# The first stage of an attention and gated-MLP kernel on one core, its order of work changed

## The chip, the cores and the metric

The kernel runs on one core of a Trainium2 chip. The core has a matrix engine (TensorE, PE in the profile), a vector engine (VectorE, DVE), an activation engine (ScalarE, ACT), a general engine (GpSimd, POOL) and a synchronising engine (SyncE, SP) that here only issues transfers. Each engine takes its instructions in the order in which they were written; semaphores hold an instruction back until what it needs is there. The metric is the device time of one execution in microseconds, lower is better.

## The reference

For 8 batches, 8 heads, 576 positions and 64 numbers per head: attention in which a position sees its neighbours up to 32 away, 8 global positions see everything, and everything sees them; then a gated feed-forward block over all 4608 tokens.

```python
scores = scale * np.matmul(q, k.transpose(0, 1, 3, 2))
mask = np.abs(pos[:, None] - pos[None, :]) <= 32
mask = mask | is_global[:, None] | is_global[None, :]
attn = softmax(np.where(mask, scores, -1e9))
x = (attn @ v).transpose(0, 2, 1, 3).reshape(4608, 512)
ffn = gelu(x @ w_gate) * (x @ w_val) @ w_out          # 512 -> 1536 -> 512
out = x + sigmoid(x @ w_res) * ffn
```

## The kernel before

The 4608 tokens are cut into 9 chunks of 512, and each batch into 9 windows of 64 positions, so a chunk has 8 windows. From chunk to chunk the feed-forward matmuls of one chunk run on TensorE while the attention of the next is made beside them. Only the first chunk has nothing to run beside: the first 28 us or so of the kernel are its attention, and the change is there. The schedule is written out by hand; the order of the calls in the source is the order on each engine.

What happens in this first stage, with the names used in the code:

- SyncE's queue (and two transfers on ScalarE's) loads q and k of batch 0 in five parts (head pairs 0 to 3 and a tail called -1), then V in five parts, then the weights as pieces of 512 KB (`load_piece`), each into a free staging place. SyncE issues in order and waits for earlier transfers as it goes.
- `cast_raw` turns a part of q or k into bfloat16: parts 0 and 1 on VectorE (k) and ScalarE (q), the rest on GpSimd. `turn_pair` transposes it on TensorE (`tk`, `tq` in PSUM) and copies it out (`kt` on VectorE, `qt` on ScalarE).
- `first_masks` makes `isg` in PSUM, and from it `hide`, which a matmul adds to the scores; `other_masks` makes `nong`, `row_masks` makes `maskr` (two instructions) from `far`, `nong` and `hot`. `one_hot` tiles (`picked`, `held_end`, `picked_end`) pick the global rows out of k and q by matmuls (`pick`); `own`, `vgb` and `gt` are constants and padding for the global rows.
- `first_scores(quad, pp)` makes two banks of local scores (four windows, two head pairs) and takes their exponential into `pt` (`weigh`, ScalarE).
- `global_scores`, `global_exp` and `global_rows` make the scores of the 8 global rows, their exponential (`ptg`, `gt`), multiply `gt` by `maskr` (VectorE), sum over all keys into `sn`, and spread the sum by head into `vgs` (VectorE, two instructions for batch 0).
- V is cast by GpSimd into `ve` (five parts); `vo` is the same shifted by 64 rows, made by copies between partition halves.
- `local_values(0, t)` multiplies `pt` with V for two windows; `global_values` adds the global part from `gt` and `vgs`; `norm` divides (VectorE) into `xtok`; `turn_x` transposes (`tx`) and copies to `xt` (ScalarE for t = 0, 1, 2, VectorE for t = 3).
- `begin(t, js)` multiplies the 128 columns of token block t with the first two column blocks of the gate and value weights; after it the feed-forward loop runs with 512 columns at a time.
- GpSimd casts the weight pieces 0, 1, 2 ... (`cast_piece`) as they land; piece 0 is for gate, piece 1 for value.

Of the kernel before, what the change touches and what calls it, by code (L numbers as in the profile page):

```python
# [13 lines left out]
ALU = mybir.AluOpType  # L14


def view(t, p0, pn, off, dims):

    step = t.ap[0][0]
    return bass.AP(tensor=t.tensor, offset=t.offset + p0 * step + off, ap=[[step, pn]] + dims)  # L20
# [3 lines left out]
def kernel(  # L24
# [12 lines left out]
    nc = tc.nc  # L37
    B, H, S, D = q.shape
# [99 lines left out]
    def staged(n):  # L138
        return slots[turn_of[n]].rearrange("p (a b) -> p a b", b=pieces[n][1].shape[2])
# [1 line left out]
    def load_piece(n):  # L141
        nc.sync.dma_start(staged(n), pieces[n][0])

    def cast_piece(n, copy):
        copy(pieces[n][1], staged(n))  # L145

# [102 lines left out]
    def zero_v(i, eng):  # L251
        eng.memset(ve[i][:, :, :, D:VG], 1.0)
        eng.memset(ve[i][0:32, 0, :, :], 0.0)
        eng.memset(ve[i][96:128, 4, :, :], 0.0)

    def zero_gt(i, eng):
        eng.memset(gt[i][:, 0:64], 0.0)
        eng.memset(gt[i][:, 64 + S:128 + S], 0.0)
# [87 lines left out]
    picked = const.tile([128, RPP, NG], BF16, name="picked", tag="picked")  # L346
    picked_end = const.tile([128, RPP, H, NG], BF16, name="picked_end", tag="picked_end")
    held_end = const.tile([128, RPP, NG], BF16, name="held_end", tag="held_end")
    for n, t in enumerate((picked, held_end)):
        nc.vector.tensor_tensor(t, view(gall, 0, 128, 0, [[0, RPP], [1, NG]]),  # L350
                                view(place, 0, 128, RPP * n, [[1, RPP], [0, NG]]), ALU.is_equal)
    nc.vector.tensor_tensor(picked_end, view(held_end, 0, 128, 0, [[NG, RPP], [0, H], [1, NG]]),
                            view(low8, 0, 128, 0, [[0, RPP], [1, H], [0, NG]]), ALU.mult)
    nc.vector.memset(own[0][:, 0:16], 0.0)
    nc.vector.tensor_scalar(own[0][:, 16:128], ident[:, 0:112], ask_row, None, ALU.mult)
    nc.vector.tensor_scalar(own[1], ident, keys_row, None, ALU.mult)
    zero_gt(0, nc.vector)
    NWM = NW + 3
    maskw = const.tile([128, NWM, 64], BF16, name="maskw", tag="maskw")

# [19 lines left out]
    def other_masks():  # L380
        for hf, n in enumerate((256, 320)):
            nc.vector.tensor_single_scalar(nong[:, 256 * hf:256 * hf + n], isg[:, hf, 0:n], 0.5, ALU.is_lt)

    def row_masks():

        nc.vector.scalar_tensor_tensor(maskr, far, 1024.5, nong, ALU.is_gt, ALU.mult)
        nc.vector.tensor_tensor(maskr, maskr, hot, ALU.add)
# [1 line left out]

    twice = {what: const.tile([128, B // 2, 2, D], BF16, name=f"{what}gd", tag=f"{what}gd") for what in "kq"}  # L390
    vgb = const.tile([128, B // 2, VG], BF16, name="vgb", tag="vgb")
    nc.vector.memset(vgb[:, :, D:VG], 1.0)

    def double_qk(n0, n1):
        for what in "kq":
# [35 lines left out]
                             view(src[what], 64 * u, 64, off + 16 * e + 8 * u, [[32, NP], [1, NG]]))  # L431

    def spread_v(n0, n1):
        nc.vector.tensor_copy(vgb[:, n0:n1, 0:D], gath["v"][:, n0:n1, :])

    ring = {"n": 0}
# [54 lines left out]
    def global_exp(b, sg, ss):  # L491
        e = b % 2
        to = ptg[e].rearrange("k c r -> k (c r)")
        done = 0
        for part in ss:
            n = part.shape[1]
            nc.scalar.activation(to[:, done:done + n], part, ACTF.Exp, bias=0.0, scale=SCALE)
            done += n
        g = gt[e][:, 64:64 + S]
        nc.scalar.activation(g.rearrange("p (a c) -> p a c", a=2), sg[:, :, 0:288], ACTF.Exp, bias=0.0, scale=SCALE)  # L500
        nc.vector.tensor_tensor(g, g, maskr, ALU.mult)
# [20 lines left out]
                                    view(head8, 0, 128, 2 * p, [[2, n], [1, 2], [0, VG]]), ALU.mult)  # L522


    def first_scores(quad, pp):

        sc = [bank([128, 2, 4, 64], "sc") for _ in range(2)]
        for u in range(2):
            nc.tensor.matmul(sc[u], ident_big, view(hide, 0, 128, 256 * quad, [[0, 2], [1, 256]]), start=True, stop=False)
        heads(0, quad, pp, sc, False)  # L530
        for u in range(2):
            weigh(quad, pp, u, sc[u])

    def heads(c, quad, pp, sc, first):

# [9 lines left out]
    def weigh(quad, pp, u, sc, stay=False):  # L545
        mine = view(pt, 0, 128, ((4 * pp + u) * CH + 4 * quad) * 64, [[2 * CH * 64, 2], [64, 4], [1, 64]])
        nc.scalar.activation(sc if stay else mine, sc, ACTF.Exp, bias=0.0, scale=SCALE)  # L547
        return mine, sc if stay else mine
# [22 lines left out]
    def local_values(c, t):  # L571
        if split(c, t):
            pool, tag = (pss, "sc") if c else (psm, "mm")
            nds = [pool.tile([128, 512], F32, name=f"nd{hf}", tag=tag) for hf in range(2)]
            nd = None
        else:
            nd = psn.tile([128, 2, 512], F32, name="nd", tag="nd")
            nds = [nd[:, 0, :], nd[:, 1, :]]
        wins = [divmod(CH * c + 2 * t + e, NW) for e in range(2)]
        for h in range(H):  # L580
            for e, (b, i) in enumerate(wins):
                vw = ve[b % 2][:, i // 2, h, :] if i % 2 == 0 else vo[b % 2][:, i // 2, h, :]
                nc.tensor.matmul(nds[h // 4][64 * e:64 * e + 64, VG * (h % 4):VG * (h % 4) + VG],  # L583
                                 pt[:, h, 2 * t + e, :], vw, start=(h % 4 == 0), stop=False)
        return nd, nds, wins
# [149 lines left out]
            cast_raw(p, what, POOL)  # L735
    for p in (0, 1):
        if p:
            for what in "kq":
                turn_pair(0, p, what)
        for what in "kq":  # L740
            pick(p, what)
    other_masks()
    zero_v(0, nc.vector)
    first_scores(0, 0)
    for p in (-1, 2, 3):
        for what in "kq":
            if p == 3:
                pick(p, what)
            else:
                turn_pair(0, p, what)  # L750
        if p == 3:
            spread_picked()
        for what in "kq":
            if p == 3:
                turn_pair(0, p, what)
            else:
                pick(p, what)
        if p < 0:
            ACT(found_end, isg[:, 0, 320:448])
            first_scores(1, 0)  # L760
    sg, ss = global_scores(0)
    for c in range(2):
        cast_v(0, c, POOL)
    POOL(vo[0][64:128, 0:1, :, :], ve[0][0:64, 1:2, :, :])
    DVE(vo[0][0:64, 0:2, :, :], ve[0][64:128, 0:2, :, :])
    spread_v(0, 1)
    row_masks()
    global_exp(0, sg, ss)
    first_scores(0, 1)
    cast_v(0, 2, POOL)  # L770
    POOL(vo[0][64:128, 1:2, :, :], ve[0][0:64, 2:3, :, :])
    for c in (3, 4):
        cast_v(0, c, POOL)
    POOL(vo[0][64:128, 2:4, :, :], ve[0][0:64, 3:5, :, :])
    first_scores(1, 1)
    begun_v = [local_values(0, t) for t in range(2)]
    global_rows(0)
    ACT(vo[0][0:64, 2:4, :, :], ve[0][64:128, 2:4, :, :])

    nc.scalar.activation(none, none, ACTF.Gelu, bias=0.0, scale=1.0)  # L780
    for n in range(4):
        cast_piece(n, POOL)
        if n < 2:
            load_piece(10 + n)
        else:
            load_raw(1, "kq"[n - 2], 0, nc.sync)
        if n == 1:
            fill(band, 1.0, [([[-1, 64]], 1, 0, ALU.is_ge, 0.0), ([[1, 64]], -1, 64, ALU.is_ge, 0.0)])
# [15 lines left out]

    values(0, 2)
    turn_x(0, 0)
    values(0, 3)
    turn_x(0, 1)
    begin(0, (0,))
    turn_x(0, 2)  # L810
    begin(0, (1,))
    begin(1)
# [201 lines left out]
```

## Time and profile before

| what | value |
|---|---|
| median of 3 runs | 385.8 us (385.33 to 386.08) |
| the profiled execution | 385.43 us, of which the span of the core is 383.7 us |
| TensorE busy | 370.2 us, 96% of the span |
| VectorE, ScalarE, GpSimd busy | 200.7, 169.6 and 168.9 us |
| slices of TensorE's busy share (40 of 9.6 us) | the first is 3 tenths, the last 6, nearly all others 9 or more |

The profile is one execution. Times in it count from the start of the span. In the timeline a row has the start, the length, the engine, the line of the source, the operation, the tiles written and read, the shape and how many instructions were merged; a bracket at its end is the time that the engine stood idle before it and what ended that idleness. In the table by stretches each engine has its busy time in that stretch.

### The profile page before, as it was taken

How to read it: one execution, taken by the hardware profiler on the slowest of the kernel's cores; microseconds unless marked ns; L12 is line 12 of the kernel's file. 1: busy time of each engine (PE TensorE's matmuls, PEld its weight loads, DVE VectorE, ACT ScalarE, POOL GpSimd, SP SyncE). 2: the span in 40 equal slices, each digit the busy share in tenths (PEclk: the TensorE clock that was granted, in tenths of full speed). 3: DMA queues.
4: the chain of work that ended last, by engine and by line, in shares of the span. 5: the costliest groups of instructions: out<-in, count | busy, mean ns of one | idle time of the engine just before them, and what ended most of it. 6: DMA issues, size and time to landing. Idle time of an engine off the chain costs nothing.

```text
span 383.7 us, 8470 instructions
## 1 busy us (share of the span) xinstructions
PE 370.2 (96%) x3332; PEld 185.1 (48%) x3332; DVE 200.7 (52%) x467; ACT 169.6 (44%) x291; POOL 168.9 (44%) x203
## 2 busy tenths in 40 slices
PE   3989989999999999999999999999999999999996
PEld 2574555445544554455444544454445444444444
DVE  7767674536723573447434744564446534553322
ACT  4763685336333543355334633372338233723311
POOL 7877683868255624661366128712501210121012
PEclk9999999999999999999999999999999999999999
DMA  8999999799949943999399939994990410041002
GB/s 242 251 375 365 246 334 219 165 179 162 106 112 148 202 72 104 129 193 106 92 141 172 125 98 127 188 97 126 105 165 4 109 57 0 3 113 53 0 29 83
DMA packets 156810, 53.70 MB, mean 140 GB/s; under 512 B 140194, under 2 KB 147234, under 8 KB 156770
## 3 DMA queue, kind: packets, MB, share of 16 engines
q1 hardware_dynamic: 80832, 42.80, 46.8%
q0 software_dynamic: 75392, 9.84, 43.9%
q8 instruction: 26, 0.43, 0.5%
q10 hardware_dynamic: 546, 0.52, 0.4%
q14 instruction: 14, 0.11, 0.1%
HBM read 39.19 MB, written 9.44 MB: 127 GB/s over the span
## 4 chain that ended last, share of the span: by engine, by line
PE 84%; DMA 9%; SPq 3%; POOL 2%; issue 1%; DVE 0%; ACTq 0%; DVEq 0%; POOLq 0%
PE f_ps L703 24%; PE v_ps L647 22%; PE g_ps L647 22%; PE r_ps L673 8%; DMA extra<-in_moe_w_val_dram 5%; PE nd L583 3%; SPq L185 3%; PE sc L540 2%; DMA wo_t<-in_k_dram 2%; PE nd L596 2%; DMA xtok<-in_v_dram 2%; DMA ht<-in_q_dram 1%; POOL wo_t L145 1%; PE sg L478 1%; PE sg L485 1%
## 5 line engine op out<-in xcount | busy, mean ns | idle before, releaser
L656 DVE SCALAR_TENSOR_TENSOR ht<-gsb,v_ps 128x512 bf16<-128x512 bf16 x108 | 74.2, 688 | 97.5 <-PE v_ps L647 90.2
L653 ACT ACTIVATE gsb<-g_ps 128x512 bf16<-128x512 f32 x108 | 64.4, 597 | 121.9 <-PE g_ps L647 120.7
L709 POOL TENSOR_TENSOR ob<-prb,xtok 128x512 f32<-128x512 f32 x35 | 40.3, 1155 | 167.0 <-DVE prb L707 167.0
L647 PE MATMUL g_ps<-xt,wg_t 128*128 128x512 bf16 (+1 forms) x456 | 111.9, 368 | 0.0
L647 PE MATMUL v_ps<-xt,wv_t 128*128 128x512 bf16 (+1 forms) x456 | 111.9, 368 | 0.0
L703 PE MATMUL f_ps<-wo_t,ht 128*128 128x512 bf16 x420 | 97.9, 379 | 0.0
L647 PEld LDWEIGHTS <-wv_t 128*128 128x128 bf16 x456 | 43.5, 98 | 49.1
L647 PEld LDWEIGHTS <-wg_t 128*128 128x128 bf16 x456 | 43.4, 98 | 48.7
L703 PEld LDWEIGHTS <-ht 128*128 128x128 bf16 x420 | 40.4, 98 | 46.9
L681 ACT ACTIVATE rsb<-r_ps 128x512 bf16<-128x512 f32 x36 | 21.9, 611 | 66.5 <-PE r_ps L673 66.5
L707 DVE SCALAR_TENSOR_TENSOR prb<-rsb,f_ps 128x512 f32<-128x512 bf16 x35 | 24.1, 688 | 51.2 <-PE f_ps L703 50.4
L673 PE MATMUL r_ps<-wr_t,xt 128*128 128x512 bf16 x144 | 37.0, 381 | 1.0 <-ACT rsb L681 1.0
L547 ACT ACTIVATE pt<-sc 128x512 bf16<-128x512 f32 x64 | 33.3, 615 | 3.8 <-PE sc L540 3.8
L91 POOL DMA_DIRECT2D q_st<-in_q_dram x25 | 21.5, 866 | 18.2 <-DMA qt<-q_st 18.1
L99 POOL DMA_DIRECT2D ve<-in_v_dram x30 | 25.5, 866 | 0.0
L565 DVE TENSOR_TENSOR pt<-pt,maskw 128x512 bf16<-128x512 bf16 x56 | 21.9, 422 | 2.5 <-ACT pt L547 0.9
L91 POOL DMA_DIRECT2D k_st<-in_k_dram x25 | 21.2, 867 | 3.6 <-DMA kt<-k_st 2.9
L673 PEld LDWEIGHTS <-xt 128*128 128x128 bf16 x144 | 12.3, 98 | 15.8 <-issue 3.9
L583 PEld LDWEIGHTS <-pt 128*64 128x64 bf16 x576 | 11.2, 110 | 9.7 <-issue 5.0
L583 PE MATMUL nd<-ve,pt 128*64 128x65 bf16 x320 | 13.6, 196 | 0.7 <-DVE xtok L617 0.6
L617 DVE TENSOR_TENSOR xtok<-nd,rden 128x512 bf16<-128x512 f32 x20 | 13.8, 691 | 0.8
L611 DVE TENSOR_TENSOR xtok<-nd,rden 128x256 bf16<-128x256 f32 x32 | 13.6, 425 | 1.1
(174 smaller groups left out, 289.4 us busy)
## 6 DMA issues: line engine op xcount, KB each, us to landing
out_dram<-ob SPq DMA_DIRECT2D x35, 256.0 KB
vo<-ve SPq DMA_DIRECT2D x12, 260.0 KB
q_st<-in_q_dram POOLq DMA_DIRECT2D x20, 128.0 KB, 6.3
k_st<-in_k_dram POOLq DMA_DIRECT2D x20, 128.0 KB, 6.7
ve<-in_v_dram POOLq DMA_DIRECT2D x18, 128.0 KB, 7.6
wo_t<-in_k_dram SPq DMA_DIRECT2D x8, 256.0 KB
vraw<-in_q_dram SPq DMA_DIRECT2D x8, 256.0 KB
extra<-in_moe_w_out_dram SPq DMA_DIRECT2D x4, 512.0 KB
```

The lines of the kernel that those rows point to most:

```text
L91: nc.gpsimd.dma_start(dst[0:n, r, :].rearrange("p (h d) -> p h d", d=D), src[b].rearrange("h s d -> s h d")[128 * r:128 * r + n])
L99: nc.gpsimd.dma_start(t[p0:p1, c, :, 0:D], v[b].rearrange("h s d -> s h d")[s0 + p0:s0 + p1])
L547: nc.scalar.activation(sc if stay else mine, sc, ACTF.Exp, bias=0.0, scale=SCALE)
L565: nc.vector.tensor_tensor(m, x, view(maskw, 0, 128, 64 * i0, [[0, 2], [64, 4], [1, 64]]), ALU.mult)
L583: nc.tensor.matmul(nds[h // 4][64 * e:64 * e + 64, VG * (h % 4):VG * (h % 4) + VG], pt[:, h, 2 * t + e, :], vw, start=(h % 4 == 0), stop=F ...
L647: nc.tensor.matmul(held[what][:, c0:c1], w[:, kk, 128 * j:128 * j + 128], x[:, kk, c0:c1], start=(kk == 0), stop=(kk == NKT - 1))
L653: nc.scalar.activation(held["s"], held["g"], ACTF.Gelu, bias=0.0, scale=1.0)
L656: nc.vector.scalar_tensor_tensor(ht[:, j, :], held["s"], 0.5, held["v"], ALU.mult, ALU.mult)
L673: nc.tensor.matmul(r_ps, xt[c % 2][:, kk, 128 * t:128 * t + 128], wr_t[:, kk, :], start=(kk == 0), stop=(kk == NKT - 1))
L703: nc.tensor.matmul(held["f"], ht[:, j, 128 * t:128 * t + 128], wo_t[:, j, :], start=(j == 0), stop=(j == NFF - 1))
L707: nc.vector.scalar_tensor_tensor(prb, held["r"], 1.0, held["f"], ALU.add, ALU.mult)
L709: nc.gpsimd.tensor_tensor(ob, prb, xtok[c % 2][:, t, :], ALU.add)
```

## The change

In the helper `cast_piece` a range of columns can be given. The one-hot tiles for the tail, the `own` constants and the padding of `gt` become functions that are called later: after the picks of the pairs 0 and 1 and (for `own`) after `zero_v`. `other_masks` is called between the turns of pair 0 and pair 1, `row_masks` after the tail's pick, before the scores of quad 1. The exponential of `first_scores(0, 1)` is called after `global_exp`, which itself comes after the V casts and copies; the last V copy goes from ScalarE to VectorE and up ahead of `global_exp`; `global_rows(0)` comes ahead of the two `local_values`. The casts of the weight pieces 0 and 1 are cut into two halves of 128 columns. `begin(0, (0,))` moves ahead of `values(0, 3)` and `turn_x(0, 1)`.

```diff
+    def cast_piece(n, copy, n0=0, n1=None):
+        copy(pieces[n][1][:, :, n0:n1], staged(n)[:, :, n0:n1])
...
-    for n, t in enumerate((picked, held_end)):
-        nc.vector.tensor_tensor(t, view(gall, ...), view(place, ...), ALU.is_equal)
-    nc.vector.tensor_tensor(picked_end, view(held_end, ...), view(low8, ...), ALU.mult)
-    nc.vector.memset(own[0][:, 0:16], 0.0)
-    nc.vector.tensor_scalar(own[0][:, 16:128], ident[:, 0:112], ask_row, None, ALU.mult)
-    nc.vector.tensor_scalar(own[1], ident, keys_row, None, ALU.mult)
-    zero_gt(0, nc.vector)
+    def one_hot(t, n): ...            # the same is_equal
+    def one_hot_end(): ...            # held_end, then picked_end
+    def own_rows(): ...               # own[0], own[1], zero_gt(0)
+    one_hot(picked, 0)
...
-    nc.vector.memset(vgb[:, :, D:VG], 1.0)
...
     def spread_v(n0, n1):
+        if n0 == 0:
+            nc.vector.memset(vgb[:, :, D:VG], 1.0)
...
     for p in (0, 1):
         if p:
+            other_masks()
             for what in "kq":
                 turn_pair(0, p, what)
         for what in "kq":
             pick(p, what)
-    other_masks()
+    one_hot_end()
     zero_v(0, nc.vector)
+    own_rows()
     first_scores(0, 0)
...
             ACT(found_end, isg[:, 0, 320:448])
+            row_masks()
             first_scores(1, 0)
     sg, ss = global_scores(0)
...
+    spread_v(0, 1)
     DVE(vo[0][0:64, 0:2, :, :], ve[0][64:128, 0:2, :, :])
-    spread_v(0, 1)
-    row_masks()
-    global_exp(0, sg, ss)
-    first_scores(0, 1)
+    late = first_scores(0, 1, False)
...
     POOL(vo[0][64:128, 2:4, :, :], ve[0][0:64, 3:5, :, :])
+    DVE(vo[0][0:64, 2:4, :, :], ve[0][64:128, 2:4, :, :])
+    global_exp(0, sg, ss)
+    for u in range(2):
+        weigh(0, 1, u, late[u])
     first_scores(1, 1)
+    global_rows(0)
     begun_v = [local_values(0, t) for t in range(2)]
-    global_rows(0)
-    ACT(vo[0][0:64, 2:4, :, :], ve[0][64:128, 2:4, :, :])
...
     for n in range(4):
-        cast_piece(n, POOL)
+        if n < 2:
+            for j in range(2):
+                cast_piece(n, POOL, 128 * j, 128 * j + 128)
+        else:
+            cast_piece(n, POOL)
...
     values(0, 2)
     turn_x(0, 0)
+    begin(0, (0,))
     values(0, 3)
     turn_x(0, 1)
-    begin(0, (0,))
     turn_x(0, 2)
```

## Rows read from the trace of the kernel before

**Rows 1.** Busy time by stretch: length, then each engine's busy time, clock, DMA
```profile
0.00:23.70 23.70, 15.62 (x288) 10.56 (x289) 18.46 (x76) 14.54 (x26) 18.87 (x37) 1.00 1.03 269
23.70:46.90 23.20, 23.18 (x195) 13.98 (x193) 14.86 (x39) 11.31 (x21) 17.07 (x22) 1.00 1.09 330
```
**Rows 2.** Timeline of TensorE in the first stage: start, length, instruction, idle before
```profile
6.64 0.61 PE L450 MATMUL tk<-ident,k_st 128*128 128x128 bf16 x4 [0.86 <-DVE k_st L270]
...
13.60 0.40 PE L450 MATMUL tk<-ident,k_st 128*128 128x128 bf16 x4
...
15.58 0.64 PE L485 MATMUL sg<-qt,kgz 128*32 128x288 bf16 x8 [0.51 <-DVE qgz L422]
...
20.47 0.83 PE L596 MATMUL nd<-vgs,gt 128*128 128x260 bf16 x4 [0.53 <-DVE vgs L520]
...
22.86 0.22 PE L583 MATMUL nd<-ve,pt 128*64 128x65 bf16 x1 [0.55 <-DVE xtok L617]
...
24.82 0.39 PE L647 MATMUL g_ps<-xt,wg_t 128*128 128x128 bf16 x4
...
27.90 1.02 PE L647 MATMUL g_ps<-xt,wg_t 128*128 128x512 bf16 x4
```
**Rows 3.** Timeline of VectorE, the first masks and k casts
```profile
5.40 0.42 DVE L352 TENSOR_TENSOR picked_end<-held_end,low 128x256 bf16<-128x256 bf16 x1
5.75 0.40 DVE L355 TENSOR_SCALAR own<-ident,nums 128x112 bf16<-128x112 bf16 x1
...
6.17 0.42 DVE L270 CAST k_st<-wo_t 128x512 bf16<-128x512 f32 x1
...
7.16 0.53 DVE L270 CAST k_st<-wo_t 128x512 bf16<-128x512 f32 x1
```
**Rows 4.** Timeline of VectorE, from the tail's copy to the global sums
```profile
11.66 0.87 DVE L455 COPY kt<-tk 64x256 bf16<-64x256 bf16 x2
14.04 0.69 DVE L457 COPY kt<-tk 128x512 bf16<-128x512 bf16 x1 [1.50 <-PE tk L450]
...
17.02 0.75 DVE L386 SCALAR_TENSOR_TENSOR maskr<-xtok,nong 128x576 bf16<-128x576 f32 x1
17.80 0.75 DVE L387 TENSOR_TENSOR maskr<-maskr,hot 128x576 bf16<-128x576 bf16 x1
18.65 1.12 DVE L501 TENSOR_TENSOR gt<-gt,maskr 128x576 bf16<-128x576 bf16 x1
19.99 0.76 DVE L520 TENSOR_TENSOR vgs<-sn,head 128x260 bf16<-128x260 f32 x2 [0.22 <-PE sn L516]
```
**Rows 5.** Timeline of VectorE, later, beside GpSimd's weight casts and V copies
```profile
33.94 0.90 DVE L396 CAST kgd<-kgf 128x128 bf16<-128x128 f32 x1
...
52.25 0.46 DVE L501 TENSOR_TENSOR gt<-gt,maskr 128x576 bf16<-128x576 bf16 x1 [0.27 <-ACT gt L500]
```
**Rows 6.** Timeline of GpSimd: gathers, casts of q and k, V copy, weight casts, V of batch 1
```profile
4.76 1.39 POOL L327 DMA_INDIRECT vgf<-in_v_dram,idx  x1 [0.87 <-DVE ghot L337]
6.45 0.99 POOL L327 DMA_INDIRECT kgf<-in_k_dram,idx  x1 [0.30 <-issue]
...
8.70 0.62 POOL L267 CAST k_st<-wo_t 128x512 bf16<-128x512 f32 x1
...
11.49 0.61 POOL L270 CAST q_st<-ht 128x512 bf16<-128x512 f32 x1
...
18.30 1.16 POOL L774 COPY vo<-ve 64x1040 bf16<-64x1040 bf16 x1
...
21.17 1.04 POOL L145 CAST wv_t<-extra 128x1024 bf16<-128x1024 f32 x1 [0.37 <-DMA extra<-in_moe_w_val_dram]
...
33.72 1.04 POOL L145 CAST wv_t<-extra 128x1024 bf16<-128x1024 f32 x1 [0.32 <-DMA extra<-in_moe_w_val_dram]
```
**Rows 7.** Timeline of ScalarE: exponential of the global rows, copy of the first token block
```profile
17.26 0.65 ACT L500 ACTIVATE gt<-sg 128x576 bf16<-128x576 f32 x1
...
22.36 0.57 ACT L628 COPY xt<-tx 128x512 bf16<-128x512 bf16 x1
```

More of the change, by code (lines that the diff above doesn't have):

```diff
@@ L142, in load_piece @@
         nc.sync.dma_start(staged(n), pieces[n][0])
-    def cast_piece(n, copy):
-        copy(pieces[n][1], staged(n))
+    def cast_piece(n, copy, n0=0, n1=None):
+        copy(pieces[n][1][:, :, n0:n1], staged(n)[:, :, n0:n1])
     RPP = 4
@@ L348, with one_hot, one_hot_end, own_rows @@
     held_end = const.tile([128, RPP, NG], BF16, name="held_end", tag="held_end")
-    for n, t in enumerate((picked, held_end)):
+    def one_hot(t, n):
         nc.vector.tensor_tensor(t, view(gall, 0, 128, 0, [[0, RPP], [1, NG]]),
                                 view(place, 0, 128, RPP * n, [[1, RPP], [0, NG]]), ALU.is_equal)
-    nc.vector.tensor_tensor(picked_end, view(held_end, 0, 128, 0, [[NG, RPP], [0, H], [1, NG]]),
-                            view(low8, 0, 128, 0, [[0, RPP], [1, H], [0, NG]]), ALU.mult)
-    nc.vector.memset(own[0][:, 0:16], 0.0)
-    nc.vector.tensor_scalar(own[0][:, 16:128], ident[:, 0:112], ask_row, None, ALU.mult)
-    nc.vector.tensor_scalar(own[1], ident, keys_row, None, ALU.mult)
-    zero_gt(0, nc.vector)
+    def one_hot_end():
+        one_hot(held_end, 1)
+        nc.vector.tensor_tensor(picked_end, view(held_end, 0, 128, 0, [[NG, RPP], [0, H], [1, NG]]),
+                                view(low8, 0, 128, 0, [[0, RPP], [1, H], [0, NG]]), ALU.mult)
+    def own_rows():
+        nc.vector.memset(own[0][:, 0:16], 0.0)
+        nc.vector.tensor_scalar(own[0][:, 16:128], ident[:, 0:112], ask_row, None, ALU.mult)
+        nc.vector.tensor_scalar(own[1], ident, keys_row, None, ALU.mult)
+        zero_gt(0, nc.vector)
+    one_hot(picked, 0)
     NWM = NW + 3
@@ L522, in global_rows, with first_scores @@
                                     view(head8, 0, 128, 2 * p, [[2, n], [1, 2], [0, VG]]), ALU.mult)
-    def first_scores(quad, pp):
+    def first_scores(quad, pp, now=True):
         sc = [bank([128, 2, 4, 64], "sc") for _ in range(2)]
@@ L530, in first_scores @@
         heads(0, quad, pp, sc, False)
-        for u in range(2):
+        for u in range(2 if now else 0):
             weigh(quad, pp, u, sc[u])
+        return sc
     def heads(c, quad, pp, sc, first):
```

## The prediction

> **What bounds the kernel now.** I read the engine table first: TensorE is busy for 370.2 of 383.7 us, and the slices say that only the first of 9.6 us is far from full. So the whole kernel ends earlier or later by what the first stage moves TensorE's start into its unbroken work. The table by stretches says where that is: 15.62 us busy in the first 23.7 us, then 23.18 of 23.20 [rows 1]. TensorE's timeline then gives the holes of the first stage and who ended them: the first k cast (until 6.64), the spread of the global rows (until 15.58), the global sums `vgs` (until 20.47) and the division of token block 1 (until 22.86); the first 512-column matmul, at 27.90, is the mark by which I count [rows 2]. Every one of these holes ends on VectorE, which is busy 18.46 of 23.7 us [rows 1]; so I read VectorE's queue row by row, and beside it GpSimd's, because some VectorE rows are longer than their work.
>
> **A wait between VectorE and GpSimd that the change walks into.** The product of `gt` with its mask takes 0.46 us in batch 1 and 1.12 us in batch 0 [rows 4, 5]. In batch 0 it starts at 18.65 inside GpSimd's copy of V (18.30 to 19.46) and ends 0.31 us behind that copy [rows 4, 6]. The cast of `kgd`, 128 numbers a row, takes 0.90 us and ends at 34.84, 0.08 us behind GpSimd's weight cast (33.72 to 34.76) [rows 5, 6]. So a VectorE instruction that reads two tiles in SBUF, or casts from SBUF to SBUF, waits for the GpSimd instruction that runs, and does its work then. [...]
>
> **The change part by part.**
>
> *Start.* `held_end`, `picked_end`, `own` and padding leave the queue ahead of the first k cast, which now starts at 6.17 [rows 3] and could start about 5.2. That would be 0.9 us. But GpSimd's first gather runs from 4.76 to 6.15, and the `own` product inside it took 0.40 us for 112 numbers and ended with it; the second k cast (0.53 against 0.42 us) ends 0.25 us behind the second gather's end at 7.44 [rows 3, 6]. So I let the first k cast wait too and end 0.25 us behind 6.15, at 6.40 instead of 6.59: a gain of 0.2 us. Bounds: 0.2 and 0.95. [...]
>
> *The moved constants.* They now stand behind the copy of pair 1, which I place at 9.0 to 9.8, `nong` (0.8 us, moved into the hole before it) costing nothing. From 8.70 to 12.10 GpSimd casts six parts without a break, the first and the last of them in [rows 6], about 0.56 us apart. `held_end` waits for the cast that ends near 9.85 and ends at 9.9; `picked_end` waits for the next and ends at 10.7; `zero_v` runs to 11.6; `own[0]` waits to 11.8; `own[1]` for the last cast, to 12.3. So the tail's copy, at 11.66 before [rows 4], starts at 12.3: 0.6 us late. Without any wait it would be at 11.05, which is the other bound.
>
> *Row masks.* Two instructions of 0.75 us [rows 4]; the second held a wait, as its shape took 0.46 us for `gt`. Behind the tail's copy they run from 13.2 to 13.9 and, behind the V cast that the first held up, from 14.4 to 14.7. The hole that they aim at, 1.50 us before the copy at 14.04 [rows 4], starts 0.6 us later and is too short: the copy of pair 2 starts at 14.65, 0.6 us late, and with it the spread, the copy of pair 3 and the global scores, at 16.2 for 15.58 [rows 2], and the exponential of `gt`, which ends at 18.5 for 17.91 [rows 7].
>
> *What the move gives back.* VectorE has 1.5 us less in front of the `gt` product. `vgb` and the two V copies (about 1.3 us with one wait) fit before 18.5. The product starts at 18.55, again inside the GpSimd copy of V (now about 18.3 to 19.3), and ends at 19.6 for 19.77. `global_rows` ahead of `local_values`: its matmuls need the last V cast (18.0), `ptg` and a bank that the first late exponential frees (19.0); they end by 19.55, hidden under the product. So `vgs` starts at 19.64 instead of 19.99 [rows 4]: 0.35 us gained. Local values fill the time to 20.1; they need the second late exponential, 19.5, and are not late. The V copy on VectorE takes 1.06 us off ScalarE, where the load of the Gelu table hides it anyway: the copy of block 0 waits for its transposes.
>
> *`begin` ahead of `values(0, 3)`.* It is meant for the hole of 0.55 us before 22.86 [rows 2]. But it needs `xt` of block 0, which ScalarE copies from 22.36 to 22.93 [rows 7], later than the hole's end. So TensorE waits for ScalarE and then runs 0.45 us of `begin` (8 matmuls of 128 columns at 0.056), and `values(0, 3)` comes at 22.93 + 0.05 + 0.45 - 0.35 = 23.08 for 22.86. Behind it 0.45 us are saved, but the next block's copy (another 0.57 us) is then what `begin(1)` waits for: 24.75 for 24.82 [rows 2]. The move by itself costs 0.28 us; bounds: a gain of 0.45 if the copy were early, a loss of 0.45.
>
> *Weights in halves.* Four casts of 0.61 for two of 1.04 us: 0.4 us more GpSimd time at the most. The value piece lands at about 21.1 (its cast waits for it until 21.17 [rows 6]), so the halves of piece 0 hide before it, and its second half ends at 22.35, two microseconds before it is used. Nothing; if uncovered, 0.3 us. The loads of pieces 10 and 11 wait for these casts, but SyncE reaches them later, held by earlier transfers.
>
> **Sum.** -0.35 + 0.28 is -0.07; I take -0.1 us at the mark 27.90. TensorE is unbroken behind it, so it goes through. The profiled execution of 385.43 becomes 385.3; that is 0.37 below the median of 385.8, so the median becomes **385.7 us**.
>
> The clock is a bound of its own. [...] TensorE had been working since 6.64 with breaks below a microsecond when it rose, near 13.2. [...] I put 0.4 us either way.
>
> **Rivals.**
>
> *A, faster: the holes are as empty as they look.* No wait for GpSimd. Then the first k cast ends at 5.6, scores and turns come 0.9 us earlier, the masks fit before the copy of pair 2 (13.4), the `gt` product starts at 17.5, before GpSimd's copy, and `vgs` is bound by the sums at 18.4. The local values then bound (to 19.4), -1.15 us at block 0's division, +0.28 for `begin`: **384.9 us** (-0.87). For it: the bracket of 1.50 us in [rows 4], `picked_end` unstretched [rows 3]. Against it: the 1.12 and 0.90 us. A middle case belongs here, in which only the `gt` product slips in front of GpSimd's copy.
>
> *B, slower: VectorE's queue around the masks.* Same mechanism, worse order: six instructions each wait a whole GpSimd cast (0.56 us), where I let four wait, and some of them partly. Then the copy of pair 2 comes 1.6 to 1.8 us late instead of 0.6, and the chain of exponentials behind it (0.5 us each) ends at 20.6; the local values of the second half wait for it and pass `vgs`. It decides from 1.2 us late on. At 1.8 late local values end at 20.9 for 20.1, which with `begin` gives +0.9: **386.7 us**.
>
> *C: gain swallowed later.* With 0.9 us gained, the weight casts (one per 1.36 us, bound by transfers) and batch 1's V could be late. Stretch two has no break [rows 1], and its casts are ahead by more than that as I read them; if it holds, A turns into -0.4, 385.4 us, within my likeliest case's range.
>
> **How the numbers follow.** The likeliest case (with C) has 0.43 and its own range is 385.1 to 386.4. A has 0.36, B 0.21. What this kernel's measurement can tell from no change is 0.2%, 0.77 us: faster is below 385.03, slower above 386.57. The range for 8 in 10 reaches to A's 384.9 with 0.3 for the clock, and past B's 386.7 with half as much: 384.6 to 386.9, a tenth left out on either side. Chances: faster 0.36, same 0.43, slower 0.21.
>
> **What would show it.** In the changed profile: the first k cast ends near 6.4 (A: 5.6); `own[1]` and `picked_end` longer than alone; the copy of pair 2 at 14.65 (A: 13.4, B: 15.8); the `gt` product over 0.9 us and ending near GpSimd's copy's end; a wait of TensorE for ScalarE before the first `begin`; the first 512-column matmul at 27.8 (A: 27.0, B: 28.8). The prediction is wrong if that matmul moves by more than 0.8 us, or if it doesn't and the end does.

## The result and the profile after

The changed kernel takes 389.2 us (median of 6, 388.3 to 389.8) where the kernel before takes 385.9 beside it: ratio 1.0076, 95% interval 1.0052 to 1.010. That is 3.3 us slower by the medians (2.9 by the ratio, which goes by the means); the forecast was 385.7 (384.6 to 386.9), so the result lies 2.3 us outside its range. The profiled execution took 389.23 us with a span of 387.5 (385.43 and 383.7 before).

The same two stretches of the table by windows, after (columns as in [rows 1]):

```profile
0.00:23.70 23.70, 15.73 (x222) 9.75 (x224) 19.64 (x66) 11.65 (x22) 19.59 (x39) 1.00 1.03 274
23.70:46.90 23.20, 22.49 (x233) 13.66 (x226) 16.77 (x46) 10.33 (x20) 17.29 (x21) 1.00 1.08 326
```

TensorE is busy for as long in the first stretch as before (15.7 us), but gets through 222 instructions in place of 288: its work there is slower and later. TensorE's timeline, after, at the lines that answer to [rows 2]:

```profile
5.65 0.61 PE L459 MATMUL tk<-ident,k_st 128*128 128x128 bf16 x4
...
12.42 0.37 PE L423 MATMUL isg<-picked_end,k_st 128*128 128x64 bf16 x4 [1.32 <-DVE picked_end L356]
...
15.55 0.61 PE L459 MATMUL tk<-ident,k_st 128*128 128x128 bf16 x4
...
18.49 0.69 PE L494 MATMUL sg<-qt,kgz 128*32 128x288 bf16 x8 [0.63 <-DVE qgz L429]
...
24.10 0.80 PE L606 MATMUL nd<-vgs,gt 128*128 128x260 bf16 x4
...
26.62 0.38 PE L657 MATMUL g_ps<-xt,wg_t 128*128 128x128 bf16 x4 [0.67 <-ACT xt L638]
...
31.91 1.02 PE L657 MATMUL g_ps<-xt,wg_t 128*128 128x512 bf16 x4
```

Read the starts against [rows 2] as a ladder: the first transposes are 0.99 us early (5.65 for 6.64); the transposes of pair 2 are 1.95 us late (15.55 for 13.60), the global scores 2.91 (18.49), the global rows' values 3.63 (24.10), the first 512-column matmul 4.01 (31.91 for 27.90). The span ends 3.8 us late, so nothing is added behind that mark. So the early gain and 2.9 us beside it are lost between 5.7 and 18.5, and 1.1 us more from there to the mark. VectorE's timeline after, against [rows 3] and [rows 4]:

```profile
5.17 0.42 DVE L270 CAST k_st<-wo_t 128x512 bf16<-128x512 f32 x1
...
8.23 0.68 DVE L466 COPY kt<-tk 128x512 bf16<-128x512 bf16 x1
8.83 2.75 DVE L351 TENSOR_TENSOR held_end<-gall,place 128x32 bf16<-128x32 f32 x1
11.61 0.76 DVE L356 TENSOR_TENSOR picked_end<-held_end,low 128x256 bf16<-128x256 bf16 x1
...
13.35 0.38 DVE L361 TENSOR_SCALAR own<-ident,nums 128x112 bf16<-128x112 bf16 x1
...
13.64 0.65 DVE L362 TENSOR_SCALAR own<-ident,nums 128x128 bf16<-128x128 bf16 x1
...
14.28 0.83 DVE L464 COPY kt<-tk 64x256 bf16<-64x256 bf16 x2
15.15 1.06 DVE L394 SCALAR_TENSOR_TENSOR maskr<-xtok,nong 128x576 bf16<-128x576 f32 x1
16.24 0.75 DVE L395 TENSOR_TENSOR maskr<-maskr,hot 128x576 bf16<-128x576 bf16 x1
17.03 0.69 DVE L466 COPY kt<-tk 128x512 bf16<-128x512 bf16 x1
...
18.47 0.69 DVE L466 COPY kt<-tk 128x512 bf16<-128x512 bf16 x1
...
21.45 0.75 DVE L510 TENSOR_TENSOR gt<-gt,maskr 128x576 bf16<-128x576 bf16 x1
23.58 0.43 DVE L529 TENSOR_TENSOR vgs<-sn,head 128x260 bf16<-128x260 f32 x1 [1.38 <-PE sn L525]
```

`held_end`, 32 numbers a row, takes 2.75 us; it is also the first long piece in the chain of work that ended last. GpSimd's timeline after, over the same time, the first, the fifth and the last of six casts that follow each other without a break:

```profile
8.70 0.62 POOL L267 CAST k_st<-wo_t 128x512 bf16<-128x512 f32 x1
...
10.92 0.60 POOL L270 CAST k_st<-wo_t 128x512 bf16<-128x512 f32 x1
11.48 0.60 POOL L270 CAST q_st<-ht 128x512 bf16<-128x512 f32 x1
```

`held_end` starts behind the first cast's start and is done at 11.57, just past the end of the fifth cast (10.92 + 0.60); `picked_end` is done at 12.36, past the end of the sixth (12.08). So it missed four boundaries between casts. The two take 3.5 us in place of 0.6, and VectorE has hardly any free time from there to the copy of pair 2: 17.03 less the 2.9 lost is 14.1, its old 14.04. Without the wait that copy would not be late. With it, the row masks also find no hole any more (1.50 us before 14.04 in [rows 4]) and stand in the way. The copy of pair 3 comes next; in the kernel before it is

```profile
15.55 0.69 DVE L457 COPY kt<-tk 128x512 bf16<-128x512 bf16 x1
```

and after it comes at 18.47: of the 4.01 us at the mark, 2.92 are lost by this copy and 1.09 behind it.

The second part is TensorE's clock. In the trace's clock records the level 1.00 begins at 13.21 before and at 23.43 after; that is its rise. (Ahead of the first such record the clock column of the table shows 1.00 too, so there the level is read from the rows.) In rows: the four transposes at 15.55 still take 0.61 us, with starts 0.107 us apart, as at 6.64 in [rows 2], where before they took 0.40, with starts 0.056 apart, from 13.60 on. One more pair of rows, the last score work ahead of the global sums, before:

```profile
17.60 0.60 PE L529 MATMUL sc<-xt,ident_big 128*128 128x512 bf16 x2
18.14 0.41 PE L540 MATMUL sc<-qt,kt 64*128 64x64 bf16 x16
```

and after:

```profile
21.18 1.03 PE L538 MATMUL sc<-xt,ident_big 128*128 128x512 bf16 x2
22.15 0.61 PE L550 MATMUL sc<-qt,kt 64*128 64x64 bf16 x16
```

The two rows span 0.95 us before and 1.58 after. There are two such groups ahead of the sums, so 1.3 us more, and TensorE is what `vgs` waits for there (1.38 us in the row at 23.58).

### The profile page after: what moved, and what is told of

Read it like the earlier page. It is cut to its first block, busy times and chain, and to the rows that moved or that the text cites. A ratio compares the mean times of both kernels' runs of the same rounds, so it can differ in the third digit from the quotient of the medians.

```text
span 387.5 us, 8471 instructions
## 1 busy us (share of the span) xinstructions
PE 373.6 (96%) x3332; PEld 186.4 (48%) x3332; DVE 207.0 (53%) x468; ACT 168.5 (43%) x290; POOL 169.2 (44%) x205
## 4 chain that ended last, share of the span: by engine, by line
PE 86%; DVE 4%; DMA 3%; issue 2%; POOL 2%; ACT 2%; DVEq 0%; POOLq 0%
PE f_ps L713 23%; PE g_ps L657 22%; PE v_ps L657 21%; PE r_ps L683 8%; PE nd L593 3%; PE sc L550 3%; PE nd L606 2%; DMA q_st<-in_q_dram 2%; DMA kt<-k_st 1%; POOL ve L99 1%; PE sg L487 1%; PE sg L494 1%; DVE held_end L351 1%; PE sn L525 1%; PE tx L637 0%
## 5 line engine op out<-in xcount | busy, mean ns | idle before, releaser
L91 POOL DMA_DIRECT2D k_st<-in_k_dram x25 | 21.1, 865 | 4.1 <-DMA kt<-k_st 2.5
L550 PEld LDWEIGHTS <-kt 64*128 64x128 bf16 x576 | 10.4, 98 | 8.9 <-issue 6.0
L550 PE MATMUL sc<-qt,kt 64*128 64x64 bf16 x576 | 13.4, 196 | 1.3 <-DVE kt L464 1.1
```

Source lines behind the costliest of these rows:

```text
L91: nc.gpsimd.dma_start(dst[0:n, r, :].rearrange("p (h d) -> p h d", d=D), src[b].rearrange("h s d -> s h d")[128 * r:128 * r + n])
L550: nc.tensor.matmul(sc[u][:, m, n, :], kt[b % 2][64 * u:64 * u + 64, 2 * pp + m, 64 * i:64 * i + 128], qt[b % 2][64 * u:64 * u + 64, 2 * pp ...
```

## Experiments

Times are medians; each ratio is to runs of the kernel before on the same chip (385.3 to 385.6).

**The two one-hots alone.** The kernel before, `held_end` and `picked_end` moved and nothing else:

```
     other_masks()
+    one_hot_end()
     zero_v(0, nc.vector)
```

> The kernel before with one edit alone: held_end and picked_end move behind the picks of pairs 0 and 1. Theory T (GpSimd's unbroken run of casts, 8.70 to 12.1, keeps VectorE out until it ends; the late tail then breaks TensorE's work and its clock rises later): held_end lasts over 1.5 us, TensorE waits about 0.5 us for picked_end, the end is 0.5 to 3 us later than before (386.4 to 389). Rival R (each instruction waits for one cast at most; the loss is made by the row masks and by begin): held_end under 0.6 us, the end within 0.5 us of before.

Measured: 387.51, ratio 1.0047 (1.0016 to 1.0078). In the profile `held_end` took 1.13 us from 9.85, `picked_end` 1.31, and TensorE waited 0.93 for it. By the median these two instructions alone cost about 2 us, but the five runs lie apart: 385.6, 385.9, 387.5, 387.6 and 388.5. The one profiled is the second of these; in it the mark is at 28.91, 1.0 us late, and the span 0.5 us longer than before.

**The two one-hots back.** The changed kernel with them at their old place, behind `picked`:

```
     one_hot(picked, 0)
+    one_hot_end()
```

> The changed kernel with held_end and picked_end back ahead of the first k cast, all else as changed. Theory T: the wait of 1.3 us for picked_end is gone, the copy of the tail comes near 12, the clock rises near 13, and at least 2 of the 3.3 us come back: 386 to 387. Rival R (row masks and begin make the loss): under 1 us comes back: above 388.2.

Measured: 386.37, ratio 1.0005 (0.9986 to 1.0023): 2.8 of the 3.3 us are back. The ten runs lie from 384.5 to 387.1, and the one profiled is the slowest, with the mark at 30.11 and a clock that rose at 14.30 and fell from 17.71 to 21.12. The `own` products are now the ones that meet the casts, as VectorE's timeline of this kernel shows:

```profile
10.28 1.34 DVE L361 TENSOR_SCALAR own<-ident,nums 128x112 bf16<-128x112 bf16 x1
...
11.54 1.21 DVE L362 TENSOR_SCALAR own<-ident,nums 128x128 bf16<-128x128 bf16 x1
```

**Sources in PSUM.** Same place in the queue, but both instructions are copies that read PSUM and nothing in SBUF; the kernel leaves out the tail's one-hots:

```
     def one_hot_end():
+        nc.vector.tensor_copy(held_end.rearrange("p a b -> p (a b)"), isg[:, 0, 0:RPP * NG])
+        nc.vector.tensor_copy(picked_end.rearrange("p a b c -> p (a b c)"), isg[:, 1, 0:RPP * H * NG])
```

> The changed kernel, in which the two instructions of the tail's one-hots (held_end, picked_end) are copies of 32 and 256 numbers out of PSUM at the same place of VectorE's queue; the one-hots of the tail are left out, so its global rows are not the reference's. L (what holds them is that they read two tiles in SBUF while GpSimd reads SBUF): both run at once, about 0.2 and 0.4 us, and are over by 9.7 (12.36 in the changed kernel). The two own products then meet GpSimd's casts as they did with the one-hots back at their old place (1.34 and 1.21 us), so the first 512-column matmul comes near 28 to 29 and the time near 386.4 (385.6 to 387.1). Q (it is their place in the queue, behind the copy of pair 1, whatever they read): they still end near 12, TensorE waits over a microsecond for picked_end, time 388.5 to 389.5.

Measured: 386.36, ratio 1.0016 (1.0 to 1.0032); the run profiled took 386.9, and its mark is at 29.76, later than was expected, with a clock that fell from 18.61 to 22.02. VectorE's timeline:

```profile
9.27 0.19 DVE L355 CAST held_end<-isg 128x32 bf16<-128x32 f32 x1 [0.37 <-PE isg L422]
9.38 0.41 DVE L356 CAST picked_end<-isg 128x256 bf16<-128x256 f32 x1
...
10.77 0.78 DVE L360 TENSOR_SCALAR own<-ident,nums 128x112 bf16<-128x112 bf16 x1
...
11.47 1.20 DVE L361 TENSOR_SCALAR own<-ident,nums 128x128 bf16<-128x128 bf16 x1
```

GpSimd casts without a break here too (8.67 to 12.06). With PSUM as the source the pair is unstretched (0.19 and 0.41 us); the products behind it, which read SBUF, are held (0.78 and 1.20). So the place in the queue does not make the wait; what the instruction reads does, and the same 2.8 us come back. It does not take two full tiles: the `own` products read one, and a single number a row.

**Breaks between the casts.** The changed kernel, a memset of one column on GpSimd behind each of the six casts:

```
             cast_raw(p, what, POOL)
+            nc.gpsimd.memset(gap, 0.0)
```

> The changed kernel with a GpSimd memset of one column behind each of the six casts of q and k. Theory T, first half (VectorE is kept out because the casts follow each other without a break in reading SBUF): held_end falls from 2.75 to under 0.8 us, and 1 to 3 us of the loss come back. Rival F (held_end waits for something else than the running casts): held_end stays above 2 us and the time within 0.5 us of the changed kernel.

Measured: 389.11, ratio 1.0091 (1.0065 to 1.0116), no gain. VectorE's timeline:

```profile
8.81 0.54 DVE L351 TENSOR_TENSOR held_end<-gall,place 128x32 bf16<-128x32 f32 x1
9.39 3.10 DVE L356 TENSOR_TENSOR picked_end<-held_end,low 128x256 bf16<-128x256 bf16 x1
```

`held_end` got in at the first break, but `picked_end`, issued at 9.39 inside the next cast, passed four boundaries with a memset in each, and ended 0.3 us behind the last cast. That a break is enough was wrong.

**Unused matmuls in TensorE's waits.** Does the changed kernel lose by the clock alone?

```
+        if p < 0:
+            filler(8)
...
+        if (quad, pp) == (1, 0):
+            filler(7)
...
+    filler(4)
     sg, ss = global_scores(0)
```

> The changed kernel with matmuls whose result nothing uses (192 columns, 8 ahead of the tail's pick, 7 ahead of the scores of quad 1, 4 ahead of the global scores) in TensorE's three longest waits; nothing else moves. Theory T, second half (the late rise of the clock makes most of the loss, and it comes late because TensorE's work is broken): the rise comes near 13 as before, transposes behind it take 0.40 us, and 1.5 to 2.5 us come back: 386.7 to 387.7. Rival K (the waits themselves make the loss, the clock little): within 0.5 us of the changed kernel, or later by the fillers.

Measured: 389.19, ratio 1.0092 (1.0064 to 1.012); single runs from 386.3 to 390.5. By the median the time did not come back. The run profiled took 387.72, the third lowest of ten, so its trace stands for the lower runs only. In it the clock rose at 11.34, fell at 18.17 and rose again at 21.58, `held_end` took 2.18 us, the mark is at 30.73, and the copy of pair 3 in VectorE's timeline is

```profile
17.39 0.69 DVE L466 COPY kt<-tk 128x512 bf16<-128x512 bf16 x1
```

It is to be set beside the execution of the changed kernel further down in which `held_end` took 2.19 us and the clock rose only at 22.43: there the same copy starts at 17.32, the mark is at 30.92, and the time is 387.90. So up to this copy the clock's level changed nothing here; VectorE's queue set the time.

**Work ahead of the first stage.** The kernel before with 25 unused matmuls from 2.2 us on:

```
+    warm(11)
     gp = psm.tile([128, NG], F32, name="gp", tag="mm")
...
+    warm(14)
     nc.vector.tensor_copy(gall, gp)
```

> The kernel before with 25 unused matmuls of 128 columns on TensorE ahead of its first real work, 11 of them from about 2.2 us and 14 from about 3.6 us (written where nothing is read). K (the lower clock until 13.2 costs time, and it rises there because TensorE began its work at 6.6): the rise comes several microseconds earlier, the four transposes of pair 0 or of pair 1 take 0.40 us in place of 0.61, heads and transposes ahead of 13.2 take half their time where they bind; the first 512-column matmul at 27.0 to 27.6 (27.90) and the time 384.3 to 385.2, with less spread from run to run than the 384.4 to 387.0 of the kernel before. W (the first stage is bound by VectorE's waits whatever the clock): rise earlier, time the same, 385.3 to 385.9. F (the clock rises early and falls again in the waits that follow): slower, 386.5 or more.

Measured: 386.10, ratio 1.0019 (1.0003 to 1.0036). The rise came at 14.88, no earlier than before, and the mark at 28.55. The first step of K did not happen: being busy earlier did not raise the clock earlier here.

**Early slots.** The kernel before; the same instructions leave the place ahead of the first k cast, but none goes beside the casts (`one_hot_heads` is the product that makes `picked_end`):

```
     cast_raw(0, "q", ACT)
+    one_hot(held_end, 1)
...
+    one_hot_heads()
     for p in (0, 1):
...
+    nc.scalar.activation(own[0][:, 16:128], ident[:, 0:112], ACTF.Copy, bias=0.0, scale=ask_row)
+    nc.scalar.activation(own[1], ident, ACTF.Copy, bias=0.0, scale=keys_row)
     zero_v(0, nc.vector)
```

> The kernel before with the same instructions taken from ahead of the first k cast, but put where no cast of GpSimd runs: held_end into VectorE's wait for the masks (5.6 to 5.9), picked_end behind the copy of pair 0 (about 7.6), the two own products to ScalarE behind its copy of pair 1, small memsets behind the tail's copy; row masks and everything later as before. L (the loss was the wait for GpSimd's casts, not the leaving of the old place): no VectorE instruction but the old ones is stretched, held_end 0.19 and picked_end 0.42 us; kt of pair -1 starts at 10.9 to 11.7 and the first 512-column matmul at 27.0 to 27.9; time 384.6 to 385.6. Rival K (every such shift of the first stage moves the clock's rise and the time by microseconds): 386.5 or more in spite of unstretched instructions.

Measured: 384.57, ratio 0.998 (0.9968 to 0.9992): 0.8 us faster than before and 4.6 faster than the changed kernel. VectorE's timeline:

```profile
5.51 0.18 DVE L350 TENSOR_TENSOR held_end<-gall,place 128x32 bf16<-128x32 f32 x1
...
7.50 0.41 DVE L354 TENSOR_TENSOR picked_end<-held_end,low 128x256 bf16<-128x256 bf16 x1
...
13.59 0.69 DVE L462 COPY kt<-tk 128x512 bf16<-128x512 bf16 x1 [1.43 <-PE tk L455]
...
18.32 0.46 DVE L506 TENSOR_TENSOR gt<-gt,maskr 128x576 bf16<-128x576 bf16 x1
19.58 0.76 DVE L525 TENSOR_TENSOR vgs<-sn,head 128x260 bf16<-128x260 f32 x2 [0.81 <-PE sn L521]
```

Both one-hots are unstretched. The `gt` product is 1.0 us earlier than in [rows 4] (it ends at 18.78 for 19.77), but `vgs` only 0.4: the sums wait for the last cast of V, and that for its load, in GpSimd's timeline:

```profile
18.47 0.78 POOL L190 CAST ve<-vraw 96x512 bf16<-96x512 f32 x1 [1.46 <-DMA vraw<-in_v_dram]
```

The early slots together with the unused matmuls ahead:

> Both of the two kernels before this one together. K: the two gains add, first 512-column matmul at 26.2 to 27.2, time 383.6 to 384.9. W: like the early slots alone. F: slower than the early slots alone by a microsecond or more.

Measured: 386.01, ratio 1.002 (1.0 to 1.0039). The rise came at 7.23, but at 20.89 the clock fell, until 24.30, and the mark is at 28.29 for 27.50. (With the same unused matmuls and the rise at 14.88, TensorE had stood idle for 0.86 us before its first transposes at 6.67; here these follow at 5.67 without a wait.) F holds: the early rise is worth little, since TensorE then waits for others (0.73 us for the last cast of V, and `vgs` is at 19.59 for 19.58), and the mark is lost behind that, where the clock falls.

**The other parts, one by one, on top of the early slots** (384.57):

> The early slots (384.57 against 385.33 of before) and one part of the change more: the global rows' sums ahead of the local values of blocks 0 and 1 on TensorE. My step (the sums come ahead under VectorE's product, vgs 0.35 us earlier): 384.0 to 384.5. Rival V (the sums' last matmuls wait for the last cast of V, which in the early slots waited 1.46 us for its load and ended at 19.25; the local values, 0.9 us of work, are then queued behind that wait): TensorE idle for 0.5 to 1 us ahead of the sums, 384.6 to 385.3.

The global sums first: 384.56, ratio 0.9984 (0.9971 to 0.9997). `vgs` comes at 19.28 for 19.58 and the mark at 27.32 for 27.50, but the time shows no gain: it lies between the two forecasts.

> The early slots and the row masks at the changed kernel's place, behind the tail's copy, in VectorE's hole of 1.43 us ahead of the copy of pair 2. L (two instructions of 0.75 us, or 0.46 where nothing is in their way): the copy of pair 2 starts at 13.6 to 13.9 (13.59), the product of gt 0.3 to 0.9 us earlier, under 18; the time 384.2 to 384.8, since vgs waits for the sums either way. Rival B (each waits a whole cast of V): the copy of pair 2 at 14.5 or later, 385.3 to 386.

The row masks in the hole: 385.14, ratio 1.0001 (0.9989 to 1.0012). In its profile the masks took 0.72 and 0.75 us, the copy of pair 2 came at 13.64 and the `gt` product at 17.55, 0.77 earlier; `vgs` stood at 19.61 for 19.58. The hole holds the masks, and nothing waits for them. Neither forecast has the time: its profile, with the mark at 27.52 for 27.50, does not show what the 0.57 us between the two medians are; their intervals just touch.

> The early slots and begin of block 0 ahead of the values of block 3, as in the changed kernel. My step: TensorE waits about 0.6 us for ScalarE's copy of xt where it waited 0.55 for the division, and the mark moves by +0.28: 384.7 to 385.1. Rival (the work of 0.45 us fits the hole): 384.0 to 384.4.

`begin` ahead: 385.28, ratio 0.9999 (0.9987 to 1.0012), 0.7 us slower than the early slots and later than the forecast. The mark moved by 0.23 us (27.73), near the forecast 0.28; the rest of the loss lies behind the mark. The copy that it needs, in ScalarE's timeline:

```profile
21.80 0.59 ACT L633 COPY xt<-tx 128x512 bf16<-128x512 bf16 x1
```

and the matmul that waits for it, in TensorE's (the row names GpSimd's `band`, long done; the copy ends at 22.39):

```profile
22.44 0.38 PE L652 MATMUL g_ps<-xt,wg_t 128*128 128x128 bf16 x4 [0.67 <-POOL band L224]
```

> The early slots with the global sums ahead and the row masks at the changed kernel's place together. My step: with the product of gt earlier the sums' turn counts, so more than the two apart: 383.6 to 384.4. Rival V (the load of V bounds the sums): 384.5 to 385.3.

Sums first and masks in the hole together: 384.74, ratio 0.9987 (0.9974 to 0.9999), in rival V's range. `vgs` at 19.02 and the mark at 26.99, 0.5 us before the early slots' own; but the span ends 0.3 us behind theirs. One place where it goes is in TensorE's timeline, a wait that is 0.41 us in the early slots:

```profile
52.97 1.02 PE L678 MATMUL r_ps<-wr_t,xt 128*128 128x512 bf16 x3 [0.73 <-ACT rsb L686]
```

**Does the end follow the clock?** Four more profiled executions of two programs from above, first the two one-hots alone, twice, then the changed kernel, twice:

> The kernel before with the two tail one-hots alone moved, another look (its runs went from 385.6 to 388.5; in the one profiled, the clock rose at 11.67, the first 512-column matmul came at 28.91 and the span was 384.2). K (the spread is the clock): where the rise comes later than 15 or the clock falls again ahead of 25, the first 512-column matmul comes at 30 or later and the span is 385.5 or more; where it rises near 12, 28.9 and 384.2 again. Rival (the spread has another cause): 28.6 to 29.2 whatever the rise.

> The same kernel as in the look before this one, one look more. K: rise late or a fall ahead of 25, first 512-column matmul at 30 or later; rise near 12, 28.9. Rival: 28.6 to 29.2 whatever the rise.

> The changed kernel, another look (clock rose at 23.43, first 512-column matmul at 31.91, span 387.5). K: if the rise comes ahead of 16, the first 512-column matmul comes by 30.5 and the span is under 386.3; if it comes again past 22, 31.6 to 32.2 and 387.2 to 387.9. Rival: 31.6 to 32.2 whatever the rise.

> The changed kernel, one look more. K: rise ahead of 16, first 512-column matmul by 30.5 and span under 386.3; rise past 22, 31.6 to 32.2 and 387.2 to 387.9. Rival: 31.6 to 32.2 whatever the rise.

One-hots alone (385.94 us above; 386.05 and 385.83 here): rise at 11.67, 12.12, 14.20, mark at 28.91, 29.02, 28.74. All rise early, so they do not decide between K and its rival. The wait was not the same in them: `held_end` took 1.13, 1.05 and 0.18 us, `picked_end` 1.31, 0.42 and 0.42, and still `picked_end` ended near one time (12.33, 12.01, 11.87), because what stands before it came later. In the last of them GpSimd waited for a load between two casts (11.04 to 11.48), and `held_end` came into that gap, in VectorE's and GpSimd's timelines:

```profile
11.23 0.18 DVE L351 TENSOR_TENSOR held_end<-gall,place 128x32 bf16<-128x32 f32 x1
...
11.48 0.86 POOL L270 CAST k_st<-wo_t 128x512 bf16<-128x512 f32 x1 [0.44 <-DMA wo_t<-in_k_dram]
```

`picked_end` runs from 11.45 to 11.87, unstretched; this time it is GpSimd's cast, begun 0.03 us behind it, that takes 0.86 us for 0.61.

Changed kernel, in order of the rise: 22.43, 23.43, 25.08, with the mark at 30.92, 31.91, 32.80 and the span 386.2, 387.5, 388.3. The mark follows, but so does VectorE's queue. In the execution with the earliest rise `held_end` got in one cast sooner:

```profile
8.82 2.19 DVE L351 TENSOR_TENSOR held_end<-gall,place 128x32 bf16<-128x32 f32 x1
11.04 0.75 DVE L356 TENSOR_TENSOR picked_end<-held_end,low 128x256 bf16<-128x256 bf16 x1
...
13.31 0.84 DVE L464 COPY kt<-tk 64x256 bf16<-64x256 bf16 x2
...
17.32 0.69 DVE L466 COPY kt<-tk 128x512 bf16<-128x512 bf16 x1
```

From this one to the profile above, the copy of pair 3 moves by 1.15 us (17.32 to 18.47) and the mark by 0.99: VectorE's queue accounts for all of it. In the one with the latest rise the whole stage starts 0.46 us later (first k cast at 5.63 for 5.17) and the copy of pair 3 0.44 (18.91), the mark 0.89; here about half goes along with the rise. No execution of the changed kernel as it is had a rise ahead of 22.

The two programs meet at one point, the tail's copy, which starts at 13.31 above and with the one-hots alone at

```profile
13.31 0.88 DVE L461 COPY kt<-tk 64x256 bf16<-64x256 bf16 x2
...
16.45 0.69 DVE L463 COPY kt<-tk 128x512 bf16<-128x512 bf16 x1
```

From the same start the changed kernel's mark is 2.0 us later (30.92 for 28.91): 0.87 up to the copy of pair 3, where its row masks stand in VectorE's queue, and 1.14 behind it, where its clock is still low until 22.43. So a late tail costs more together with the other parts of the change than alone.

## Why the prediction was wrong, step by step

*What bounds the kernel* was right: the end moved by what the mark at 27.90 moved, 3.8 us for 4.0.

*Start*: put at 0.2 us, it is 1.0. The first k cast took 0.42 us at 5.17, inside GpSimd's gather (4.76 to 6.15 before and after): it was over before the gather's end and was not held. With the one-hots back the same cast started at 5.73 and ran over the end of that gather, and then it was:

```profile
5.73 0.65 DVE L270 CAST k_st<-wo_t 128x512 bf16<-128x512 f32 x1
```

It ended 0.24 us behind the gather (6.14), as the prediction had put it. So the reading of the long `own` row in [rows 3] was right for what runs at a gather's end, and the step failed in taking the whole gather for it. Held by the whole gather the cast would have waited; the 0.42 us decide against that for the first part of a gather, the 0.65 us agree for its end. The bound of 0.95 was the answer, and the mark 5.6 of rival A came true.

*The moved constants* is the step that failed. It rests on the sentence that an instruction "waits for the GpSimd instruction that runs, and does its work then". That gave one cast of 0.56 us for each. The 1.12 and 0.90 us that taught it in [rows 4, 5] both lay beside a single long GpSimd instruction and could not show what a run of six does. Measured: `held_end` missed four boundaries, `picked_end` ended 1.7 us later than put (12.36 for 10.7), and the tail's copy started 2.0 us later than put. That the two engines hold each other up is right: with sources in PSUM the pair takes 0.19 and 0.41 us in place of 2.75 and 0.76, and GpSimd's cast that began behind `picked_end` took 0.86 us for 0.61. But by one cast at a time the wait would be at most 0.6 us, a cast's own length, and 2.75 and 3.10 us are measured.

*Row masks*: the copy of pair 2 was put at 14.65 and came at 17.03. Most of that is inherited: the tail's copy alone was 2.0 us later than put. On top of the early slots the masks fit the hole to 0.05 us. Behind a late tail they don't, as the step says: with the tail's copy at 13.31 in both, the copy of pair 2 starts at 14.93 with the one-hots alone and at 15.88 in the changed kernel, 0.69 us behind the end of its transposes (15.19). So the 0.6 us charged were right in kind and near in size; only the start was put too early.

*What the move gives back* (-0.35) is 0.0 in time as far as it was run; the V copy on VectorE and the later exponential were not run by themselves. (The load of the Gelu table is a row of 1.28 us on ScalarE, at 20.96 before and at 23.89 after; after it the copy of block 0, at 25.99, waited 0.60 us for its transposes, as the prediction had put it.) In the trace the sums first and masks together bring `vgs` 0.56 us earlier; a part is then waited off at later places. The load of V, which bounds the sums once VectorE is early, was seen only as a time for its cast (18.0), not as a bound.

*`begin` ahead*: sign, cause and size right at the mark (+0.23 for +0.28; the wait for ScalarE is 0.67 us). The time grew by 0.7, and where the rest goes behind the mark was not found. *Weights in halves*: no effect seen; they were not run by themselves.

*The clock*: put at 0.4 us either way, an estimate of the author's that no run shows. What the runs show in its place: in the changed kernel the rise was 10 us later (23.43 for 13.21), and the last score work ahead of the sums took 1.3 us more, about three times the 0.4; of each microsecond of that work 0.4 us is the late rise (1.58 us for 0.95). It does not add to the wait ahead of the copy of pair 3: there the runs with an early and a late rise agree (17.39 and 17.32).

*Rivals.* B had the mechanism and the place next to it: VectorE's queue behind casts, decided by lateness past 1.2 us. Its price of 0.56 us an instruction made 386.7 out of what is 389.2. A's first half held: the start was free. With no wait it gives 384.9, and the early slots measured 384.6; that is near by luck, since they hold neither the masks' move nor `begin`, and `vgs` stood at 19.58 where A has 18.4. C's kind of loss is there: the sums and masks together lose their gain behind the mark, but at a wait for ScalarE, not at the casts that C names.

**What stays open.** The mark's 4.01 us are 2.92 in VectorE's queue up to the copy of pair 3 and 1.09 behind it; how these 1.09 come out of the low clock (1.3 more for the score work), the wait before `begin` and what the move gives back was not separated. Whether the wait makes the clock rise late: undoing the wait moves the rise with it, and nothing here sets the rise alone. Why runs of one program lie apart (385.6 to 388.5 for the two one-hots alone, 386.3 to 390.5 with the unused matmuls), while the profiled ones are mostly of one kind. What lets VectorE in at one boundary between casts and not at the others.

## What to carry to other kernels

Before an instruction that reads SBUF is moved on VectorE, look at what GpSimd runs at the new place, and count a run of back-to-back instructions as one: the bound of the wait is the end of the run, not of the instruction at hand (2.75 and 3.10 us here, past four boundaries each). Small constants go where GpSimd casts nothing, or onto ScalarE; beside a gather they were free here when they were over before its end (`picked_end` took 0.42 us at 5.40 in [rows 3], gather to 6.15). The kernel before with the same constants moved so gained 0.8 us, where the changed kernel lost 3.3. A hole on VectorE is worth filling only if what is filled in was the last to be waited for: the masks left the critical queue and `vgs` did not move, because the sums behind V's late load were next. And a late instruction is priced with all that stands behind it in its queue: the masks were free behind an early tail and cost 0.7 us behind a late one.

## What the runs showed of the hardware that was not expected

VectorE stayed held through several boundaries of GpSimd's casts: 2.75 us past four of them, and 3.10 us past four even with another instruction of 0.1 us in each. A gap in which GpSimd waited 0.44 us for a load let it in, and then GpSimd's cast was the one to take longer (0.86 us for 0.61).

A gather of GpSimd's held VectorE only at its end. The first k cast took 0.42 us in every profile in which it was over before the gather's end, and 0.65 in the one in which it was not (5.73 to 6.38, gather to 6.14); the `own` product that ended with the gather in [rows 3] took 0.40 us, and 0.24 at 5.16 in the kernel with the two one-hots alone moved.

TensorE's clock also falls again inside the first stage. In the changed kernel with the one-hots back, the table by windows (PEclk is its third column from the end) shows it between 17.7 and 21.1, behind a wait of 1.41 us for VectorE that ended at 17.01:

```profile
14.30:17.70 3.40, 1.89 (x43) 1.38 (x40) 3.25 (x9) 1.92 (x4) 3.21 (x5) 1.00 1.16 288
17.70:21.10 3.40, 3.36 (x53) 1.60 (x53) 2.75 (x5) 2.06 (x4) 2.35 (x4) 0.50 1.08 348
```

Unused work on TensorE didn't help: 25 matmuls ahead of the first stage left the rise at 14.88 in one kernel, brought it to 7.23 with a fall at 20.89 in the other, and both were slower than without (by 0.8 and 1.4 us).
